# One strip of an expert transfer sent as sixteen transfers of eight rows, in a slot-attention, soft-MoE and softplus-MLP kernel

## The chip, the cores and the metric

The kernel runs on one core of a Trainium2 chip. The metric is the device time of one execution in microseconds (us): 570.08 us, the median of three runs (569.05, 570.08 and 570.2).

## The reference

Three blocks follow each other. An attention over 32 memory slots for each of 8 batches and 8 heads gives x of 4608 rows by 512. A soft mixture of eight experts then reads x through 32 slots, and each expert multiplies its four slots by two matrices of 2 MB each:

```python
slot_input = d.T @ x                      # d: softmax over all rows of x @ phi
for e in range(E):                        # E = 8
    h = np.maximum(slot_input[e] @ w1[e], 0.0)      # w1[e]: 512 x 1024
    slot_out[e] = h @ w2[e]                         # w2[e]: 1024 x 512
x = c @ slot_out                          # c: softmax over the slots
g = np.maximum(h, 0.0) + np.log1p(np.exp(-np.abs(h)))   # h = x @ w_in
return g @ w_out
```

The expert matrices are 32 MB, the largest input. They are multiplied with only 32 slot rows, so their cost is that of loading them.

## The kernel before

The kernel has three stages. In the first the attention is computed and reduced to the 32 slot inputs (`SX`). In the second the experts are applied. In the third, some 390 us long, the softplus MLP runs over all 4608 rows; TensorE's matrices there are built from `soT`, which comes out of the last product of the second stage.

The sixteen expert matrices lie in HBM in the order of their use, as eight blocks `moe_w[0]` to `moe_w[7]` of 128 rows by 8192 floats (4 MB, two matrices side by side, 32 KB in a row). `expert_loads` (L1052) brings each block into one of four buffers of 4 MB (`both`, the pool `w32`); blocks 0 to 6 are one transfer each, block 7 is four (2 MB, 1 MB, 512 KB and 512 KB). Block 4 holds `w1` of experts 4 and 5, and takes the buffer of block 0. All loads are issued by SyncE's queue (SP) in the order of the program: two pairs of MLP weights, the eight blocks, then the other MLP weights (L1109, L1118).

`first_layer` (L1278) computes an expert's hidden rows (`hid`, L1285) and transposes them (`hTp`, L1301); `second_layer` (L1309) adds its output to two banks of PSUM (`S`, L1318), in the order of the experts. The last of these products releases `slot_out` (`sop`, L1342), and with it the third stage (L1544 and after). Where the planner expected TensorE to wait, it put in products of zeros (`idle`, L956), a number that is fixed when the program is built.

The order of instructions on every engine is fixed by the planner `Flow`, which simulates times when the program is built. The transfers of SP take eight completion semaphores in turn (DMAHW0 to DMAHW7, called lanes here). SP starts a transfer on a lane only when the transfer before it on that lane, eight transfers back, has landed. These waits are written by the layer under the kernel and not in its text, and they stand in the program's order.

Of the kernel before, what the change touches and what calls it, by code (L numbers as in the profile page):

```python
# [283 lines left out]
def tile_slot_attention_soft_moe_softplus_mlp(  # L284
# [10 lines left out]
    nc = tc.nc  # L295
# [698 lines left out]
    for pr in range(NPR):  # L994
        r = 20 * pr
# [56 lines left out]
    def expert_loads():  # L1052

        order = [(w, e + i) for e in range(0, NE - 4, 2) for w in ("w1", "w2") for i in range(2)]
        order += [("w1", NE - 4), ("w1", NE - 3), ("w2", NE - 4), ("w1", NE - 2)]
        order += [("w1", NE - 1), ("w2", NE - 3), ("w2", NE - 2), ("w2", NE - 1)]
        for n in range(NE):
            pair = order[2 * n : 2 * n + 2]
            ends = [0, 8192] if n < NE - 1 else [0, 4096, *(4096 + y for _, y in LAST_PARTS)]
            for a, b in zip(ends, ends[1:]):  # L1060
                yield [("D", 0.03 + 9.7 * (b - a) / 8192)], [] if a else ["+w32"], 0
                if a == 0:
                    i = flow.got["w32"]
                    both = w32[i].tile([128, 8192], F32, tag="w32", name="w")
                    for k, (kind, e) in enumerate(pair):
                        at[kind, e] = i
                        views(kind, e, both[:, 4096 * k : 4096 * k + 4096])
                nc.sync.dma_start(out=both[:, a:b], in_=moe_w[n][:, a:b])
                for k, (kind, e) in enumerate(pair):
                    arrived_w(kind, e, a - 4096 * k, b - 4096 * k)  # L1070

# [10 lines left out]
    def views(kind, e, t):  # L1082
        if kind == "w1":
            for n in range(2):
                w1_t[e, n] = t[:, 2048 * n : 2048 * n + 2048].rearrange("p (k f) -> p k f", k=KC)
            return
        for n in range(2):
            w2_t[e, n] = t[:, 2048 * n : 2048 * n + 2048].rearrange("p (h k d) -> p h k d", h=2, k=4)

    def arrived_w(kind, e, a, b):  # L1090
        if kind == "w1":
            done(f"w1{e}")
            return
        for n in range(2):
            for half in range(2):
                if a <= 2048 * n + 1024 * half < b:
                    done(f"w2{e}{n}.{half}")
# [28 lines left out]
    def weight_loads():  # L1126
        early = list(EARLY)
        for _ in range(early_at.count(-1)):
            x = early.pop(0)
            yield from load_wi(x[1]) if x[0] == "wi" else load_wo(x[1])  # L1130
        yield from expert_loads()
        for x in early + LATE:
            yield from load_wi(x[1]) if x[0] == "wi" else load_wo(x[1])
# [129 lines left out]
    def runs(units):  # L1263

        n = len(groups(units))
        if n == 1:
            return [(q, 0) for q in "1265734"]
        return [("2", 0), ("1", 0), ("2", 1), ("1", 1), ("3", 0), ("3", 1), ("6", 0), ("6", 1)] + [
            ("5", 0), ("7", 0), ("7", 1), ("5", 1), ("4", 0), ("4", 1)
        ]  # L1270
# [640 lines left out]
    n = 0  # L1911
# [8 lines left out]
    for j, (where, units) in enumerate(JOBS):  # L1920
        if isinstance(where, int):
            for u in units:
                r = due[j, u] - LEAD["h"] - 1e4 * (n == 0)
                flow.add(first_h(n, list(last_h)), r, "fb")
                r = due[j, u] - LEAD["g"] - 1e4 * (n == 0)
# [14 lines left out]
        r = due[j, runs(units)[0][0], 0] - LEAD["x"]  # L1940
# [104 lines left out]
```

## Time and profile before

| | |
|---|---|
| median of three runs | 570.08 us |
| the profiled execution | 569.04 us |
| its span | 567.3 us |
| PE busy | 544.3 us, 96% of the span |
| DVE busy, ACT busy | 461.4 us, 373.5 us |
| DMA from SP | 96.80 MB |

The span is cut into 40 slices of 14.2 us in the page's second part; a digit is the busy share of a slice in tenths. PE is TensorE, DVE VectorE, ACT ScalarE, SPq the queue of SyncE that issues transfers, PEld TensorE's load of the stationary matrix. A transfer's time to landing runs from the start of its issue to its completion.

### The profile page before, as it was taken

Reading aid. Unit: us, or ns where it says so; the run is one execution under the profiler, and the core shown is the slowest. Engines: PE = TensorE matmul, PEld = TensorE weight load, DVE = VectorE, ACT = ScalarE, POOL = GpSimd, SP = SyncE. Lnnn points to the kernel's source line nnn. Section 1 sums busy time; section 2 is a strip of 40 time slices with the busy share of each in tenths; the row PEclk is TensorE's granted clock in tenths of the full one; section 3 lists DMA queues with packets and bytes.
Section 4 is the critical chain, followed back from the end, with each engine's and each line's share of the span. In section 5 each row is a group of like instructions: output and inputs, shape, how many; then the busy total and the mean of one; then the engine's idle time right before and its main releaser. Section 6 shows DMA issues by size and latency. Waiting matters only on the chain.

```text
span 567.3 us, 10017 instructions
## 1 busy us (share of the span) xinstructions
PE 544.3 (96%) x4054; PEld 418.2 (74%) x4062; DVE 461.4 (81%) x596; ACT 373.5 (66%) x527; POOL 61.1 (11%) x76
## 2 busy tenths in 40 slices
PE   8789989998799999999999999999999999999997
PEld 4556766544447888888888888888888888888885
DVE  4578989888815998999999999999999758778953
ACT  3567866334413898588967976886887976765520
POOL 1000000000000001001023121322112110211100
PEclk9899999999899999999999999999999999999999
DMA  8999999999999476558599876899669554766842
GB/s 354 429 418 433 415 420 438 427 429 432 424 411 406 176 222 150 194 158 185 230 221 151 158 125 103 150 153 182 99 101 157 92 87 74 118 113 119 160 87 111
DMA packets 22078, 132.05 MB, mean 233 GB/s; under 512 B 2960, under 2 KB 4624, under 8 KB 16656
## 3 DMA queue, kind: packets, MB, share of 16 engines
q1 hardware_dynamic: 12528, 96.80, 41.7%
q0 software_dynamic: 9504, 34.61, 36.4%
q8 instruction: 32, 0.52, 0.4%
q14 instruction: 14, 0.11, 0.1%
HBM read 85.00 MB, written 42.47 MB: 225 GB/s over the span
## 4 chain that ended last, share of the span: by engine, by line
PE 87%; DVE 5%; DMA 3%; ACT 2%; issue 1%; SPq 0%; DVEq 0%; ACTq 0%
PE ob L1837 53%; PE ob L1691 8%; PE hp L1718 5%; DMA kv<-in_kv_dram 3%; PE idle L956 3%; PE kvp L529 3%; PE rp L609 2%; PE tp L712 2%; PE S L1318 2%; PE sc L648 1%; PE tp L484 1%; PE ob L1865 1%; PE U L859 1%; DVE arena L1192 1%; ACT a L628 1%
## 5 line engine op out<-in xcount | busy, mean ns | idle before, releaser
L1837 PE MATMUL ob<-g,WS 128*128 128x512 f32 x768 | 181.8, 389 | 0.0
L1837 PEld LDWEIGHTS ob<-g,WS 128*128 128x128 f32 x768 | 144.0, 188 | 30.2 <-issue 0.4
L1837 PE MATMUL ob<-g,W 128*128 128x512 f32 x552 | 130.5, 389 | 0.0
L1837 PEld LDWEIGHTS ob<-g,W 128*128 128x128 f32 x552 | 103.5, 188 | 21.7 <-ACT outs L837 0.2
L837 ACT ACTIVATE outs<-ob 128x1024 f32<-128x1024 f32 x78 | 80.2, 1028 | 51.4 <-PE ob L1837 40.7
L1479 POOL DMA_DIRECT2D out_dram<-outs x60 | 53.1, 919 | 451.2 <-ACT g L1782 203.0
L1784 DVE TENSOR_TENSOR g<-arena,g 128x1024 fp32r<-128x1024 f32 x61 | 74.1, 1221 | 19.7 <-ACT g L1782 19.6
L1782 ACT ACTIVATE g<-arena 128x1024 fp32r<-128x1024 f32 x61 | 64.3, 1057 | 16.6 <-PE ob L1837 13.7
L1691 PE MATMUL ob<-g,W 128*128 128x512 f32 x192 | 46.4, 390 | 0.0
L1472 DVE TENSOR_TENSOR outs<-ob,outs 128x1024 f32<-128x1024 f32 x30 | 36.7, 1223 | 11.0 <-PE ob L1837 10.8
L1691 PEld LDWEIGHTS ob<-g,W 128*128 128x128 f32 x192 | 36.0, 188 | 7.4
L1718 PE MATMUL hp<-CT,Gs 128*128 128x512 f32 x128 | 38.6, 390 | 0.0
L1784 DVE TENSOR_TENSOR g<-x,g 128x1024 fp32r<-128x1024 f32 x26 | 31.4, 1220 | 3.2 <-ACT g L1782 3.1
L956 PE MATMUL idle<-zero 128*128 128x512 bf16 x111 | 29.9, 403 | 2.5 <-POOL zero L959 1.5
L1784 DVE TENSOR_TENSOR g<-room,g 128x1024 fp32r<-128x1024 f32 x25 | 30.1, 1220 | 2.0 <-ACT g L1782 2.0
L1782 ACT ACTIVATE g<-x 128x1024 fp32r<-128x1024 f32 x26 | 27.5, 1058 | 4.4 <-PE ob L1837 2.3
L1782 ACT ACTIVATE g<-room 128x1024 fp32r<-128x1024 f32 x25 | 26.4, 1058 | 5.1 <-PE ob L1837 4.4
L1731 ACT ACTIVATE arena<-hp 128x1024 f32<-128x1024 f32 x30 | 29.6, 1019 | 0.0
L1718 PEld LDWEIGHTS hp<-CT,Gs 128*128 128x128 f32 x128 | 23.9, 188 | 5.1 <-issue 0.2
L529 PE MATMUL kvp<-kv,et 128*32 128x128 f32 x512 | 20.1, 289 | 3.0 <-DMA kv<-in_kv_dram 3.0
L956 PEld LDWEIGHTS <-zero 128*128 128x128 bf16 x119 | 11.3, 103 | 13.8 <-issue 4.6
L653 DVE TENSOR_REDUCE smx<-sc 128x16 f32<-128x512 f32 (+1 forms) x20 | 12.6, 631 | 8.2 <-PE sc L648 8.0
(202 smaller groups left out, 731.7 us busy)
## 6 DMA issues: line engine op xcount, KB each, us to landing
out_dram<-outs POOLq DMA_DIRECT2D x60, 512.0 KB, 5.4
w<-in_moe_w_dram SPq DMA_DIRECT2D x7, 4096.0 KB, 20.8
kv<-in_kv_dram SPq DMA_DIRECT2D x6, 2880.0 KB, 20.7
out_dram<-outs SPq DMA_DIRECT2D x20, 512.0 KB, 3.1
wi<-in_w_in_dram SPq DMA_DIRECT2D x8, 1024.0 KB, 18.6
wo<-in_w_out_dram SPq DMA_DIRECT2D x8, 1024.0 KB, 16.3
q<-in_q_dram SPq DMA_DIRECT2D x4, 1280.0 KB, 20.2
q<-in_q_dram SPq DMA_DIRECT2D x4, 1024.0 KB, 20.5
```

Of the source, the lines that this page charges most:

```text
L529: nc.tensor.matmul(kvp[32 * h : 32 * h + 32], lhsT=rows[:, 32 * h : 32 * h + 32], rhs=rows_of[:, c, h] if c < SC else rest[:, h], start=(c ...
L653: nc.vector.tensor_reduce(out=mx[:, cc], in_=sc[:, : len(cs)], op=ALU.max, axis=AX.X)
L837: nc.scalar.activation(o, i, AF.Copy)
L956: nc.tensor.matmul(idle[0], lhsT=zero[:, :128], rhs=zero, start=True, stop=True)
L1472: nc.vector.tensor_tensor(out=o, in0=OB[at], in1=o, op=ALU.add)
L1479: nc.gpsimd.dma_start(out=place(half, tb), in_=o, accum_op=ALU.add)
L1691: nc.tensor.matmul(bank(oc), lhsT=W[u][:, w, i, c], rhs=hb[tb, u][:, x, i], start=(fresh and i == chunks[0] and k == "0"), stop=(stop and ...
L1718: nc.tensor.matmul(hp[:, i], lhsT=Gs[:, 128 * fc : 128 * fc + 128], rhs=CTf[:, TB * tb : TB * tb + TB], start=True, stop=True,)
L1731: nc.scalar.activation(X[key][:, m], hp, AF.Softplus)
L1782: nc.scalar.activation(g[:, 0], x, AF.Copy)
L1784: nc.vector.tensor_tensor(out=g[:, 1], in0=x, in1=g.bitcast(F32)[:, 0], op=ALU.subtract)
L1837: nc.tensor.matmul(OB[at][:, t], lhsT=(W if w == "W" else WS)[u][:, x, c, cols], rhs=g[:, y, m], start=(fresh and u == grp[0] and n == 0), ...
```

## The change

Block 4 is no longer one transfer. Its first 1024 floats of each row (4 KB of 32 KB, 512 KB in all) go as sixteen transfers of eight rows each: transfer r takes rows r, r+16, ..., r+112. The other 7168 floats of each row (3584 KB) follow as one transfer. The bytes and their places in the buffer are the same.

```diff
                 if a == 0:
...
                         views(kind, e, both[:, 4096 * k : 4096 * k + 4096])
+                if n == 4:
+                    for r in range(16):
+                        nc.sync.dma_start(out=both[r::16, :1024], in_=moe_w[n][r::16, :1024])
+                    a = 1024
                 nc.sync.dma_start(out=both[:, a:b], in_=moe_w[n][:, a:b])
+                a = a if n != 4 else 0
                 for k, (kind, e) in enumerate(pair):
                     arrived_w(kind, e, a - 4096 * k, b - 4096 * k)
```

On SP the program before has, from block 2 on, these rows; `w<-in_moe_w_dram` is a block or a part of one with its rows and floats, and the brackets hold the semaphores that the instruction waits for (DMAHW is a lane, PE, DVE and Activation are engines that must be done with the buffer).

```order
L1068 DMA w<-in_moe_w_dram 128x8192 [waits DMAHW2_49,PE_49]
L1068 DMA w<-in_moe_w_dram 128x8192 [waits DVE_49,PE_49,Activation_49]
L1068 DMA w<-in_moe_w_dram 128x8192 [waits DMAHW7_49,DMAHW3_49,PE_49]
L1068 DMA w<-in_moe_w_dram 128x8192 [waits DMAHW4_49,DMAHW1_49,PE_49]
L1068 DMA w<-in_moe_w_dram 128x8192 [waits DMAHW5_49,DMAHW0_49,PE_49]
L1068 DMA w<-in_moe_w_dram 128x4096 [waits DMAHW6_49,DMAHW2_49,PE_49]
```

The third row is block 4, on lane 3. Its neighbours count on from there: block 3, the second row, is on lane 2, blocks 2, 1 and 0 are on lanes 1, 0 and 7.

On SP the changed program has seventeen rows in the place of block 4. These are the last ten of them, from the eighth piece to the rest of the block, and the row of block 5.

```order
L1070 DMA w<-in_moe_w_dram 8x1024 [waits DMAHW2_49]
L1070 DMA w<-in_moe_w_dram 8x1024 [waits DMAHW3_49]
L1070 DMA w<-in_moe_w_dram 8x1024 [waits DMAHW4_49]
L1070 DMA w<-in_moe_w_dram 8x1024 [waits DMAHW5_49]
L1070 DMA w<-in_moe_w_dram 8x1024 [waits DMAHW6_49]
L1070 DMA w<-in_moe_w_dram 8x1024 [waits DMAHW7_49]
L1070 DMA w<-in_moe_w_dram 8x1024 [waits DMAHW0_49]
L1070 DMA w<-in_moe_w_dram 8x1024 [waits DMAHW1_49]
L1070 DMA w<-in_moe_w_dram 8x1024 [waits DMAHW2_49]
L1072 DMA w<-in_moe_w_dram 128x7168 [waits DMAHW3_49]
L1072 DMA w<-in_moe_w_dram 128x8192 [waits DMAHW4_49,PE_49]
```

The eighth piece (the first row) is on lane 2, the lane of block 3. The sixteenth piece (the last but two) waits for the eighth, the rest of block 4 for the ninth, and block 5 for the tenth. The seven pieces ahead of the first row wait for transfers up to block 2, and the first of them for the buffer, as block 4 did before.

On PE the first layer of expert 4 waited for one lane before; `hid<-w,room` is its product, `S_1883<-w,hT` and `ctp` are what stands before it.

```order
L1318 MATMUL S_1883<-w,hT 32x256 x4
L1255 MATMUL ctp<-ident,c_2111 128x128 [waits DVE_49]
L1255 MATMUL ctp<-ident,c_2111 128x128 x3
L1285 MATMUL hid<-w,room 32x256 [waits DMAHW3_49]
L1285 MATMUL hid<-w,room 32x256 x15
```

On PE in the changed program the same products wait for all eight lanes, at the same place in the order.

```order
L1323 MATMUL S_1883<-w,hT 32x256 x4
L1260 MATMUL ctp<-ident,c_2127 128x128 [waits DVE_49]
L1260 MATMUL ctp<-ident,c_2127 128x128 x3
L1290 MATMUL hid<-w,room 32x256 [waits DMAHW4_49,DMAHW5_49,DMAHW3_49,DMAHW6_49,DMAHW2_49,DMAHW7_49,DMAHW1_49,DMAHW0_49]
L1290 MATMUL hid<-w,room 32x256
L1290 MATMUL hid<-w,room 32x256 [waits DMAHW3_49]
L1290 MATMUL hid<-w,room 32x256 x13
```

Before, the first product waited for the one transfer on lane 3. Now the first waits for the strip, whose sixteen pieces are on all eight lanes, and the third for the rest of the block, on lane 3 too. The order of the other engines' instructions is the same as before.

## Rows read from the trace of the kernel before

**Rows 1.** The span in 40 slices, second part of the page.

```profile
PE   8789989998799999999999999999999999999997
...
PEclk9899999999899999999999999999999999999999
DMA  8999999999999476558599876899669554766842
GB/s 354 429 418 433 415 420 438 427 429 432 424 411 406 176 222 150 194 158 185 230 221 151 158 125 103 150 153 182 99 101 157 92 87 74 118 113 119 160 87 111
```

**Rows 2.** DMA queues from 80 to 180 us: packets, bytes, share of 16 engines.

```profile
DMA packets 2795, 42.53 MB, mean 425 GB/s; under 512 B 310, under 2 KB 310, under 8 KB 566
...
q1 hardware_dynamic: 2783, 42.35, 99.9%
```

**Rows 3.** SP's issues in order of time: start us, us, line, what, number.

```profile
108.08 0.33 SPq L1068 DMA_DIRECT2D w<-in_moe_w_dram  x1
...
126.04 0.33 SPq L1068 DMA_DIRECT2D w<-in_moe_w_dram  x1
...
133.28 2.05 SPq L1068 DMA_DIRECT2D w<-in_moe_w_dram  x2
...
142.97 1.75 SPq L1068 DMA_DIRECT2D w<-in_moe_w_dram  x4
...
144.29 0.43 SPq L1068 DMA_DIRECT2D w<-in_moe_w_dram  x1
...
240.74 5.27 SPq L1428 DMA_DIRECT2D arena<-gq  x8
```

**Rows 4.** Issues at 108.08, 126.04, 144.29 and 232.02 us: KB, us to landing.

```profile
w<-in_moe_w_dram SPq DMA_DIRECT2D x1, 4096.0 KB, 24.6
...
w<-in_moe_w_dram SPq DMA_DIRECT2D x1, 4096.0 KB, 16.3
...
w<-in_moe_w_dram SPq DMA_DIRECT2D x1, 512.0 KB, 28.6
...
arena<-gq SPq DMA_DIRECT2D x1, 16.0 KB, 1.8
```

**Rows 5.** What SP waited for: us in total, times, longest us.

```profile
SPq L1068 <- PE hTp L1301: 17.9, 1, 17.9
```

**Rows 6.** DMA issues of the whole span: KB each, median us to landing.

```profile
outs<-out_dram SPq DMA_DIRECT2D x3, 512.0 KB, 3.5
arena<-gq SPq DMA_DIRECT2D x48, 16.0 KB, 3.4
```

**Rows 7.** PE in order of time: start us, us, line, operation, shape, number.

```profile
143.43 1.93 PE L1285 MATMUL hid<-w,room 128*32 128x256 f32 x32
...
153.35 3.20 PE L1318 MATMUL S<-w,hT 128*32 128x256 f32 x32
...
160.16 3.83 PE L956 MATMUL idle<-zero 128*128 128x512 bf16 x17
...
169.78 3.84 PE L1318 MATMUL S<-w,hT 128*32 128x256 f32 x64
173.55 1.33 PE L1342 MATMUL sop<-sel,s2s 128*128 128x128 f32 x8
```

**Rows 8.** PEld at the end of the second stage, idle before in brackets.

```profile
172.98 0.16 PEld L1318 LDWEIGHTS S<-w,hT 128*32 128x32 f32 x8 [0.46 <-DMA w<-in_moe_w_dram]
```

**Rows 9.** Stretches: busy us (number) of five engines, PEclk, DMA share, GB/s.

```profile
149.00:152.00 3.00, 0.88 (x6) 0.64 (x6) 2.42 (x5) 1.23 (x4) 0.00 (x0) 1.00 1.05 442
152.00:154.00 2.00, 1.60 (x12) 1.02 (x16) 1.21 (x2) 1.65 (x3) 0.00 (x0) 0.64 0.99 426
154.00:156.00 2.00, 2.00 (x25) 0.87 (x20) 1.86 (x5) 0.05 (x1) 0.00 (x0) 0.51 0.91 393
...
174.00:200.00 26.00, 26.00 (x133) 22.06 (x132) 23.09 (x30) 18.52 (x27) 0.00 (x0) 1.00 0.68 275
...
300.00:560.00 260.00, 260.00 (x1202) 214.73 (x1201) 217.58 (x208) 184.53 (x196) 48.38 (x55) 1.00 0.70 120
```

## The prediction

> **What bounds the kernel now.** I read the span in slices first. In the first 13 of the 40 slices, to 184 us, the DMA row stands at 8 and then 9 and the rate mostly above 410 GB/s; behind them the rate falls to about half and less, while PE stands at 9 to the end [rows 1]. So a stage bound by loads is followed by one bound by TensorE. The DMA queues confirm the first half: from 80 to 180 us the 16 engines are 99.9% busy with SP's transfers, at 425 GB/s [rows 2]. The stretches confirm the second: from 174 to 200 us and from 300 to 560 us PE is busy for the whole of the stretch [rows 9]. Hence the end is set by the moment at which the third stage starts, plus work that has no gap to give back.
>
> That moment hangs on block 7. Its last part is issued at 144.29 us [rows 3] and lands 28.6 us later [rows 4], at 172.9. TensorE's last weight load of the experts is released by exactly this transfer, at 172.98 [rows 8], and the product `sop`, with which the third stage begins, follows at 173.55 [rows 7]. The products of zeros ahead of it, such as the 17 at 160.16 [rows 7], are no reserve: their number is fixed, and behind them the transfer is still what is waited for. So whatever the stream of expert blocks loses before 172.9 us comes out at the end, one for one.
>
> The block in question is issued at 126.04, when SP has waited 17.9 us [rows 3, 5] for TensorE to leave the buffer. Block 3, issued at 108.08 and landing 24.6 us later at 132.7, is then still moving; block 4 lands 16.3 us after its issue, at 142.3 [rows 3, 4]. The two landings are 9.66 us apart: block 4 was queued 6.7 us ahead of its turn, and the stream had no gap. 4096 KB in 9.66 us makes 2.36 us for 1024 KB, 1.2 us for the strip of 512 KB and 8.45 us for the rest of 3584 KB.
>
> **The change, part by part.** It removes one issue of SP and adds seventeen, and it adds a wait. No bytes are added, and no engine but SP and PE has another order.
>
> *The first seven pieces.* They follow from 126.04 on. What a transfer in a row costs on SP is shown from two sides: block 7's four parts take 1.75 us, 0.44 each, and eight transfers of 16 KB take 5.27 us, 0.66 each [rows 3]. So the seven are out between 129.1 and 130.7, behind block 3, and cost nothing; the stream hides them.
>
> *The eighth piece.* It is on block 3's lane and waits until that has landed, at 132.7. SP therefore stands for 2.0 to 3.6 us, and behind it in SP's order stand eight more pieces, the rest of block 4 and blocks 5 to 7. Nothing else is queued at the DMA engines but seven pieces of 32 KB, which is 0.5 us of the stream's rate. It is this wait that ends last now: the stream runs dry.
>
> *The pieces from the eighth on.* Nine issues lie between 132.7 and the issue of the rest. At 0.44 us they take 4.0, at 0.66 us 5.9, and if each took only its own 0.33 [rows 3], 3.0. I take 0.5, 4.5 in all: they are loads like block 7's parts, which gave 0.44, but nearly all wait on a lane as the small ones do. The rest goes out at 137.2. Two more lane waits stand in this stretch, of the sixteenth piece for the eighth and of the rest for the ninth; each has eight issues, 4.0 us, to be covered by, and a small transfer lands in 1.8 to 3.4 us [rows 4, 6]. They cost nothing; at 0.44 us and 3.4 us they would just fit.
>
> *Starting the stream again.* On a quiet queue 16 KB land 1.8 us after the issue [rows 4], and 512 KB take 3.5 us [rows 6], of which 1.2 is their transport: 2.3. So between 1.8 and 2.3 us are added to the 8.45; I take 2.0. The rest of block 4 then lands at 137.2 + 2.0 + 8.45 = 147.65, against 142.3: 5.3 us late. From both sides: 132.7 + 4.0 + 1.8 + 8.45 = 146.95, 4.6 late; 132.7 + 5.9 + 2.3 + 8.45 = 149.35, 7.0 late; with 0.33 us an issue 146.0, 3.6 late.
>
> *Behind it.* Blocks 5 and 6 were issued at 133.28 and some 1.7 us later, the first part of block 7 at 142.97 [rows 3]. They now follow the rest at 137.7 and 138.2 at the earliest, well ahead of their turn at 147, so the stream has one gap and no second, and each lands 5.3 us later than before, the last at 178.2.
>
> *TensorE.* `hid` of expert 4 starts at 143.43 now [rows 7] and would start at 147.7, with the few more semaphores that it waits for beside a wait that is longer anyway. A pause of four us can cost clock: after 149 to 152 us, in which PE was busy for 0.88 of 3 us, the granted clock is 0.64 and then 0.51, about 1.2 of 2.4 GHz [rows 9], and 32 products of `S` take 3.20 us, where 64 take 3.84 later [rows 7]. If the same befell `hid`, two experts' products would grow by 2.6 us. Block 5 comes 9.66 us after block 4, and 9.9 us lie between the starts of `hid` and `S` [rows 7], of which more than 2 us, in the stretch at 149, are waits that are over by then. So I cost it at nothing; without that cover it would be 1 to 2 us.
>
> **Sum.** The profiled execution took 569.04 us, of which 567.3 is the span; 569.04 + 5.3 = 574.3. It is 1.04 us under the median of the three runs, on which the sum is 575.4. Two of the three runs lie at the upper value, so I forecast 575.0.
>
> **The rivals.** *Few engines.* If a piece of eight rows does not use all sixteen engines, its bytes pile up on some. One engine moves 32 KB in 1.21 us (4096 KB on sixteen in 9.66). On eight engines a piece is 0.15 us, under the 0.5 between issues, and nothing changes. On two, the sixteen pieces take 9.7 us, to 142.4, and the rest ends at 150.8: 8.5 late, 578.6 on the median. On one, 19.4 us: 18 late, 588. The traces hold no transfer of under 32 rows, so nothing here decides it; but what SP sends in 128 rows keeps all sixteen busy [rows 2]. The Trainium skill's page "DMA: Bandwidth & Descriptors", section "Why a DMA increments its semaphore by 16 and not by 1", says that the number of engines is the largest up to 16 that divides the slowest dimension of both sides; that is eight here, and by it the sum stays as it is. No run here shows it. Chance of two or fewer engines: 7%.
>
> *Each piece pays its landing.* If the nine pieces go one after the other, each at 1.8 us, they take 16.2 us, and block 4 lands at 159.4: 17 late, 587. Against it: eight small transfers were issued in 5.27 us, each landing in 1.8 to 3.4 [rows 3, 4, 6], so they overlap. The same page, section "Rules for kernel authors", says of transfers under 64 KB that one pays mostly overhead, which speaks against the change in either case; by the order of SP it is the issue that is paid here, not the landing. Chance 4%.
>
> *No wait that binds: not slower.* If the eighth piece's lane is free in time, SP goes through its seventeen rows from 126.04 without a stop. The stream has no gap only if the rest goes out 1.8 us ahead of 132.7, by 130.9, which needs 0.30 us an issue over sixteen; then block 4 lands at 142.3 as before, and the time is 570.1. At 0.44 the rest leaves at 133.1 and lands 1 us late, 571.1. Against it stand the lane's order and the shortest issue of 0.33 [rows 3]. Chance 4%, half of it within 0.2%.
>
> *The delay is taken up.* Transfers 5.3 us late could find time to spare further on. The last weight load's wait for the last part [rows 8] and a third stage with PE busy throughout [rows 9] speak against it; what it would take is the whole 5.3, for 570.1. Chance 3%.
>
> **How the numbers follow.** The forecast with its bounds of 3.6 and 7.0 us has 82%: 572.7 (on the lowest run, 569.05) to 577.2 (on the highest, 570.2). I draw the range from 572.8 to 578.2, since the costlier cases are likelier than the cheaper. Within 0.2%, 1.1 us, which is about what a measurement can tell from no change, lie the taken-up delay and half of the free lane: 5%. Faster needs a gain for which no row shows a source: 1%. Slower: 94%.
>
> **What would show it.** The rows of SP: seven issues from 126 us on, a pause to 132.7 that DMA of block 3 ends, nine more in some 4.5 us, and the rest at about 137. The stretch from 133 to 139 should show the DMA share far below 1, with 425 GB/s again behind it. `hid` of expert 4 should start near 148, `sop` near 179, and the third stage should be as long as before. Wrong would be: no pause of SP ahead of the eighth piece, a stream without a gap, pieces that land 10 us and more after their issue, or a `sop` that is late by much less than block 4.

## The result, and the profile after

| | median us | runs, lowest to highest | profiled execution us | its span us |
|---|---|---|---|---|
| before | 569.57 | 4, 569.01 to 570.2 | 569.04 | 567.3 |
| changed | 577.62 | 4, 576.6 to 579.09 | 576.6 | 574.8 |

The ratio is 1.0143, with a 95% interval of 1.0113 to 1.0173: slower by 6.4 to 9.9 us. The forecast was 575.0 with a range of 572.8 to 578.2. The time lies in the range, 2.6 us above the forecast. The forecast stood on a base of 570.08 us, the median of three runs; with a fourth it is 569.57, so the change itself is 8.05 us on the medians and 7.6 on the profiled executions, against 5.3 in the prediction's sum.

The span in 40 slices of the changed kernel, second part of its page; a slice is 14.4 us now.

```profile
PE   8789989998689999999999999999999999999997
...
PEclk9799999999789999999999999999999999999999
DMA  9999999995999667465599956899678555666842
GB/s 362 425 424 427 417 419 438 430 414 176 432 425 410 278 196 207 171 200 123 164 294 158 180 96 109 149 161 169 114 119 146 78 93 86 111 106 118 164 90 110
```

In the tenth slice, from 129 to 144 us, the rate is 176 GB/s; the slices on either side are at 414 and 432, and before none of the first twelve but the opening one was under 410 [rows 1]. No other slice ahead of the third stage falls out of line. The place to look at is thus the tenth slice, and SP's rows show what happens there: start us, us, line, what, and their number, of the changed kernel (L1070 is the pieces, L1072 the whole transfers).

```profile
127.00 4.42 SPq L1070 DMA_DIRECT2D w<-in_moe_w_dram  x7
...
132.89 5.43 SPq L1070 DMA_DIRECT2D w<-in_moe_w_dram  x9
...
138.36 7.42 SPq L1072 DMA_DIRECT2D w<-in_moe_w_dram  x7
```

Seven pieces go out by 131.42; then SP stands until 132.89; then nine follow, and the rest of block 4 goes out at 138.36, where the whole block was issued at 126.04 before [rows 3]. (That the pieces start at 127.00 and not at 126.04 is not the change: in this execution the first stage was 1 us longer, in its repeat below 0.2 us. Block 3 lands 0.2 us later than before.) SP's waits from 100 to 180 us (what waited, for what, us in total, times, longest) name both causes; the first is the same as before [rows 5], the second is new.

```profile
SPq L1070 <- PE hTp L1306: 17.9, 1, 17.9
...
SPq L1070 <- DMA w<-in_moe_w_dram: 1.4, 1, 1.4
```

What the stream does meanwhile stands in stretches of 1 us of the changed kernel, in the columns of rows 9.

```profile
129.00:130.00 1.00, 1.00 (x24) 0.61 (x20) 1.00 (x3) 0.50 (x3) 0.00 (x0) 1.00 0.95 365
130.00:131.00 1.00, 1.00 (x26) 0.61 (x20) 0.96 (x3) 0.30 (x1) 0.00 (x0) 1.00 0.66 229
131.00:132.00 1.00, 1.00 (x17) 0.59 (x10) 0.96 (x2) 0.00 (x0) 0.00 (x0) 1.00 0.19 62
132.00:133.00 1.00, 1.00 (x19) 0.57 (x21) 0.97 (x2) 0.86 (x3) 0.00 (x0) 1.00 0.20 57
133.00:134.00 1.00, 1.00 (x24) 0.58 (x20) 1.00 (x2) 0.32 (x2) 0.00 (x0) 1.00 0.03 12
...
138.00:139.00 1.00, 1.00 (x24) 0.65 (x20) 1.00 (x3) 0.00 (x0) 0.00 (x0) 1.00 0.14 37
139.00:140.00 1.00, 1.00 (x19) 0.50 (x8) 0.73 (x1) 0.23 (x1) 0.00 (x0) 1.00 1.80 434
140.00:141.00 1.00, 0.50 (x5) 0.26 (x3) 0.14 (x1) 1.00 (x2) 0.00 (x0) 1.00 0.17 57
```

Read the last two columns, the DMA share and the rate. A packet, one row of a transfer, is counted whole in the stretch in which it starts; that is why the share is 1.80 at 139 and 0.17 behind it. So from about 131 to 139 us hardly anything but pieces is started. In the kernel before, the stream is full from 130 to 136 us:

```profile
130.00:132.00 2.00, 2.00 (x34) 1.16 (x30) 1.93 (x3) 0.82 (x3) 0.00 (x0) 1.00 1.08 451
132.00:134.00 2.00, 2.00 (x44) 1.23 (x40) 1.97 (x4) 0.74 (x3) 0.00 (x0) 1.00 0.95 410
134.00:136.00 2.00, 1.75 (x26) 0.93 (x18) 1.93 (x3) 0.43 (x1) 0.00 (x0) 1.00 1.03 442
```

The rate falls before SP is released at 132.89, because the sixteen DMA engines do not finish block 3 together. By the packets of the changed kernel's trace, block 3's last five of 32 KB start between 130.4 and 131.0 us and end between 131.6 and 132.4; its sixteen completion signals come from 128.98 to 132.87. In the kernel before they come from 129.12 to 132.63, but there an engine that is done goes on with block 4. Here it finds only pieces.

TensorE's rows of the changed kernel carry the delay to the third stage (start us, us, line, operation, shape, number, idle before and its releaser).

```profile
149.73 3.63 PE L1290 MATMUL hid<-w,room 128*32 128x256 f32 x28 [4.71 <-DMA w<-in_moe_w_dram]
...
160.75 3.53 PE L1323 MATMUL S<-w,hT 128*32 128x256 f32 x32 [1.80 <-DMA w<-in_moe_w_dram]
...
181.25 1.19 PE L1347 MATMUL sop<-sel,s2s 128*128 128x128 f32 x8
```

The weight load that waits for the last part of block 7, in the changed kernel:

```profile
180.46 0.24 PEld L1323 LDWEIGHTS S<-w,hT 128*32 128x32 f32 x8 [0.19 <-DMA w<-in_moe_w_dram]
```

The first layer of expert 4 resumes at 149.73, released by the transfer. The last weight load comes at 180.46 instead of 172.98 [rows 8], 7.5 us late, and `sop` at 181.25 instead of 173.55 [rows 7], 7.7 us late. From `sop` to the end of the span it is 393.55 us now and was 393.75. The third stage is as dense as before [rows 9]; the changed kernel's row:

```profile
300.00:560.00 260.00, 260.00 (x1202) 214.74 (x1201) 221.89 (x213) 190.53 (x202) 49.55 (x56) 1.00 0.73 126
```

So the whole difference of the spans, 7.5 us, is lost between 127 and 150 us and handed on unchanged.

### The profile page after: what moved, and what is told of

The parts are those of the page before. It is cut to its first block, busy times and chain, and to the rows that moved or that the text cites. A ratio compares the mean times of both kernels' runs of the same rounds, so it can differ in the third digit from the quotient of the medians.

```text
span 574.8 us, 10037 instructions
## 1 busy us (share of the span) xinstructions
PE 547.9 (95%) x4054; PEld 419.8 (73%) x4062; DVE 461.5 (80%) x596; ACT 373.5 (65%) x527; POOL 61.1 (11%) x76
## 4 chain that ended last, share of the span: by engine, by line
PE 84%; DMA 11%; SPq 1%; ACT 1%; DVE 1%; issue 0%; ACTq 0%
PE ob L1842 52%; DMA w<-in_moe_w_dram 8%; PE ob L1696 8%; PE hp L1723 5%; DMA kv<-in_kv_dram 3%; PE kvp L529 3%; PE idle L956 2%; PE rp L609 2%; PE tp L712 2%; PE S L1323 1%; PE sc L648 1%; PE tp L484 1%; PE ob L1870 1%; SPq L1070 1%; ACT a L628 1%; PE U L859 1%
## 5 line engine op out<-in xcount | busy, mean ns | idle before, releaser
L1290 PE MATMUL hid<-w,room 128*32 128x256 f32 x256 | 17.7, 409 | 5.2 <-DMA w<-in_moe_w_dram 4.7
L956 PEld LDWEIGHTS <-zero 128*128 128x128 bf16 x119 | 11.4, 104 | 14.3 <-issue 5.4
```

The lines of the kernel that those rows point to most:

```text
L956: nc.tensor.matmul(idle[0], lhsT=zero[:, :128], rhs=zero, start=True, stop=True)
L1290: nc.tensor.matmul(hid[32 * j : 32 * j + 32], lhsT=SX[:, kc, NS * e : NS * e + NS], rhs=w1_t[e, j // 2][:, kc, 256 * (j % 2) : 256 * (j % ...
```

## The experiments

The theory: a transfer of SP waits for the landing of the one eight places before it. The eighth piece therefore stops SP until block 3 has landed, and the loss is that stop, the issues queued behind it and the start of a dry stream. Its rivals: small transfers move slowly (few engines, or each paying its landing), and the number or the form of the pieces costs by itself, without any stop. All kernels below change the loop of the pieces alone; everything is still loaded. The kernel before, run beside each group of them, had medians of 569.69 to 569.86 us; each ratio is taken to its own.

### Four, eight and thirty-two pieces

`e4_four_pieces` puts 32 rows, 4 apart, into each piece:

```diff
-                    for r in range(16):
-                        nc.sync.dma_start(out=both[r::16, :1024], in_=moe_w[n][r::16, :1024])
+                    for r in range(4):
+                        nc.sync.dma_start(out=both[r::4, :1024], in_=moe_w[n][r::4, :1024])
```

> The strip goes as four transfers of 32 rows, so no piece is on the lane of block 3. Lane theory (the loss is SP's stop at block 3's lane, the issues behind it at 0.61 us each and the start of the dry stream at 2.9 us): the rest is issued near 129.5 us, ahead of block 3's landing, the stream has no gap, and the time is that of before within 0.2% (569 to 570.5 us). Rival, the strip itself costs (many short rows, small transfers at the DMA engines): 1 us or more is lost here too, 571 us and above.

Measured: 569.93 us, ratio 1.0005 (0.9996 to 1.0015): no loss. SP's row of this kernel shows four issues without a stop, and two stretches of it the stream going on where the changed kernel is dry.

```profile
125.89 2.48 SPq L1070 DMA_DIRECT2D w<-in_moe_w_dram  x4
```

```profile
130.00:132.00 2.00, 2.00 (x30) 1.18 (x26) 1.93 (x3) 0.97 (x3) 0.00 (x0) 1.00 0.90 342
132.00:134.00 2.00, 2.00 (x44) 1.19 (x40) 1.97 (x4) 0.59 (x2) 0.00 (x0) 1.00 1.06 449
```

`e8_eight_pieces` has `range(8)` and `[r::8]`, 16 rows each: the first count at which a piece meets block 3's lane.

```diff
+                    for r in range(8):
+                        nc.sync.dma_start(out=both[r::8, :1024], in_=moe_w[n][r::8, :1024])
```

> The strip goes as eight transfers of 16 rows; the eighth is on block 3's lane, and only it and the rest are issued behind the stop. Lane theory: rest at 132.9 + 0.6 = 133.5 us, landing 11.3 us later at 144.8, 2.5 us late; 572 to 573 us. Rival, few engines (pieces of eight rows load eight engines unevenly): 16 rows load all sixteen alike, so the loss is gone, 570 us. Rival, the strip itself costs: half of the loss with half of the pieces, 4 us, 573.5 us.

Measured: 573.32 us, ratio 1.0065 (1.0046 to 1.0084), 3.6 us slower, 0.3 us past what was expected. By the time alone the rival that half of the pieces cost half of the loss (573.5 us) fits as well or better; the rows speak for the stop:

```profile
SPq L1070 <- DMA w<-in_moe_w_dram: 3.7, 1, 3.7
```

The eighth piece goes out only at 134.28, 1.4 us later than the eighth of the changed kernel, because block 3 landed only then (134.26); a first sign that pieces can delay the block that is still moving. That delay is larger than the excess.

`e32_thirtytwo_pieces` has `range(32)` and `[r::32]`, 4 rows each: 25 issues behind the stop.

```diff
+                    for r in range(32):
+                        nc.sync.dma_start(out=both[r::32, :1024], in_=moe_w[n][r::32, :1024])
```

> The strip goes as 32 transfers of four rows. Lane theory: 25 issues stand behind the stop instead of nine, 16 more at 0.61 us, 9.7 us more than the changed kernel: 586 to 588 us. Rival, it is the landing of a round of eight lanes that is paid (2 to 2.9 us a round) and not the issues: two more rounds, 4 to 6 us more, 581 to 583 us. Rival, few engines: four rows on four engines, 128 KB each, 4.9 us of their time, hidden or not, 577 to 582 us.

Measured: 585.02 us, ratio 1.0269 (1.0254 to 1.0284), 15.3 us slower. It fits the issues one after the other, and is 2 us and more above what rounds of landings would give. SP's row of this kernel:

```profile
133.47 13.47 SPq L1070 DMA_DIRECT2D w<-in_moe_w_dram  x25
```

25 issues in 13.47 us are 0.54 each, somewhat shorter than the 0.61 of the changed kernel, which is why the time stayed a microsecond under the expectation's lower end.

### Sixteen pieces in other forms

`again_changed` is the changed kernel, unedited, run beside the experiments.

> The changed kernel as it is, on the chip of these experiments. Lane theory: 7.5 us over before (5.5 for nine issues at 0.61, 2.9 for the start of the stream, less the 1.2 of the strip, and some 0.3 later on): 576.5 to 577.8 us.

Measured: 577.58 us, ratio 1.0139 (1.0123 to 1.0154), 7.7 us slower. The result stands. Its trace differs in where the stop ends: block 3 lands at 133.59, the eighth piece goes out at 133.60, and nine issues of 0.61 us later the rest, at 139.07.

`e16w_wide_pieces` keeps sixteen pieces of 32 KB, each as 32 adjacent rows of 1 KB:

```diff
+                        rows, cols = slice(32 * (r % 4), 32 * (r % 4) + 32), slice(256 * (r // 4), 256 * (r // 4) + 256)
+                        nc.sync.dma_start(out=both[rows, cols], in_=moe_w[n][rows, cols])
```

> Sixteen pieces of the same 32 KB and on the same lanes, but of 32 rows by 256 floats (1 KB), so that the rows divide over all sixteen engines. Lane theory: the same stop and nine issues behind it; if an issue takes 0.56 us whatever its shape, 577 to 578 us as in the changed kernel; if it was long because of the eight rows and falls to the 0.44 us of the block's parts, 1.2 us less, 576 us. Rival, few engines: the loss is gone, 570 us.

Measured: 576.74 us, ratio 1.0129 (1.0111 to 1.0147), 7.05 us slower. Block 3 lands at 133.44, and the nine issues behind the stop take 5.1 us to the rest, about 0.46 us each but for one of 1.48. With 32 rows in a piece the loss stays, so it isn't that eight rows use few engines. The DMA engines from 134.0 to 134.8 us of the changed kernel, in which one piece moves, say how many a piece uses:

```profile
DMA packets 16, 0.03 MB, mean 41 GB/s; under 512 B 8, under 2 KB 8, under 8 KB 16
```

32 KB went as 8 packets of 4 KB, with 8 short ones, the signals: eight engines. By the rule that the prediction took from the Trainium skill's page "DMA: Bandwidth & Descriptors" (section "Why a DMA increments its semaphore by 16 and not by 1") it is eight as well, and the trace agrees.

`e16c_adjacent_rows` gives piece r the rows 8r to 8r+7 instead of rows 16 apart:

```diff
-                        nc.sync.dma_start(out=both[r::16, :1024], in_=moe_w[n][r::16, :1024])
+                        nc.sync.dma_start(out=both[8 * r : 8 * r + 8, :1024], in_=moe_w[n][8 * r : 8 * r + 8, :1024])
```

> Sixteen pieces of eight rows as in the changed kernel, but of adjacent rows (8r to 8r+7) and not 16 apart. Theory that the rows' spacing makes an issue long (0.56 us for rows 4, 8 or 16 apart, 0.42 for 32 adjacent rows): issues of 0.42 to 0.44 us, the nine behind the stop take 4.2 us and not 5.5, 1.3 us less than the changed kernel: 575.8 to 576.5 us. Rival, an issue is long because of the few rows: 0.56 us again, and the changed kernel's time.

Measured: 574.54 us, ratio 1.0088 (1.0073 to 1.0103), 4.7 us slower, better than expected. SP's row of this kernel shows why:

```profile
133.28 2.99 SPq L1070 DMA_DIRECT2D w<-in_moe_w_dram  x9
```

The stop ends within 0.4 us of the same place (132.89 in the changed kernel, 133.60 in its repeat), but an issue takes 0.34 us from start to start, not 0.61. Neither the theory's 0.42 to 0.44 nor the rival's 0.56 (each a piece's own duration) was right: it is 0.29 here. The nine cost 3.0 instead of 5.5 us, and the time is 3.0 us under that of the changed kernel beside it (577.58): 2.4 of the 3.0 are the issues. The bytes and the number of pieces are unchanged: what was paid in the changed kernel is, for the larger part, the issue on SP.

### Is it the stop, or the number of pieces?

`e6_six_pieces` was to stand just under the stop, `e7_seven_pieces` just on it (there the rest of block 4 is eight places behind block 3), with pieces of adjacent rows.

```diff
+                    cuts = (0, 16, 32, 48, 64, 96, 128)
+                    for x, y in zip(cuts, cuts[1:]):
+                        nc.sync.dma_start(out=both[x:y, :1024], in_=moe_w[n][x:y, :1024])
```

```diff
+                    cuts = (0, 16, 32, 48, 64, 80, 96, 128)
+                    for x, y in zip(cuts, cuts[1:]):
+                        nc.sync.dma_start(out=both[x:y, :1024], in_=moe_w[n][x:y, :1024])
```

> The strip goes as six transfers of adjacent rows (four of 16, two of 32), the rest is the seventh on lane 1 (block 2, landed at 122.9). Lane theory: no stop, the rest goes out ahead of block 3's landing, no gap: 569.3 to 570.5 us, the same as before. Rival, every piece costs its share of the loss (0.5 us each): 572.5 us.

> One piece more than with six (six of 16 rows, one of 32), so that the rest itself comes on lane 2 and waits for block 3. Lane theory: a stop with no issue behind it but the rest's; what is left is the start of the dry stream alone, 11.4 us from issue to landing against 9.66 without a gap, 1.7 to 2.2 us: 571.3 to 572 us. Rival, it is the number of issues alone, the stop being harmless: within 0.5 us of six pieces.

Measured: 572.71 us (ratio 1.0055, 1.004 to 1.007) with six, 572.88 (1.0061, 1.0044 to 1.0078) with seven. Both expectations failed. Six pieces should have cost nothing and cost 2.9 us; seven lie within 0.5 us of six, which was the rival's condition, although SP does stop in them (3.8 us, the rest at 134.31). SP doesn't stop in the six:

```profile
125.88 2.66 SPq L1071 DMA_DIRECT2D w<-in_moe_w_dram  x6
```

but the stream behind them is slow, in these stretches of the kernel with six:

```profile
130.00:132.00 2.00, 2.00 (x30) 1.19 (x26) 1.93 (x3) 0.98 (x3) 0.00 (x0) 1.00 0.91 252
132.00:134.00 2.00, 2.00 (x44) 1.21 (x40) 1.97 (x4) 0.58 (x2) 0.00 (x0) 1.00 0.96 227
```

The DMA share is over 0.9, as in a full stream, and the rate about half: the engines are busy, and each byte takes longer: the packets of 32 KB that start between 129.5 and 133 us take 1.96 us in the median, where they take 1.22 in the kernel before. Block 3 lands at 134.61, 2.0 us later than before. That is a second cost, which I had not seen, and it spoils this comparison of six and seven. It could lie in the number of pieces or in their narrow bands of adjacent rows. The next three kernels separate the two.

`x6_six_spread` and `x7_seven_spread` have the same numbers of pieces, but every piece takes rows 4 apart, all over the 128; to get to six or seven, some of the four groups of rows go in two halves.

```diff
+                    for r, x, y in ((0, 0, 1024), (1, 0, 1024), (2, 0, 512), (2, 512, 1024), (3, 0, 512), (3, 512, 1024)):
+                        nc.sync.dma_start(out=both[r::4, x:y], in_=moe_w[n][r::4, x:y])
```

```diff
+                    for r, x, y in ((0, 0, 1024), (1, 0, 512), (1, 512, 1024), (2, 0, 512), (2, 512, 1024), (3, 0, 512), (3, 512, 1024)):
+                        nc.sync.dma_start(out=both[r::4, x:y], in_=moe_w[n][r::4, x:y])
```

> Six pieces again, but each of 32 rows four apart (two of 1024 floats, four of 512), as in the four pieces that cost nothing. With six pieces of adjacent rows nothing stopped SP, and yet 2.9 us were lost: in its trace the stream runs at 227 to 315 GB/s from 130 to 136 us. Theory, SBUF's side: pieces whose rows lie close together are written by all sixteen engines into few parts of SBUF, and slow each other and the rows of block 3 down; with rows spread out this goes, and without a stop the time is that of before: 569.2 to 570.7 us. Rival, it is the number of pieces: 572.5 us as with six adjacent ones.

> Seven pieces of rows four apart, so that the rest waits for block 3's lane and nothing but the rest is issued behind the stop. Lane theory: landing 11.4 us after the issue at 132.9, 144.3, 2.0 us late: 571.4 to 572.4 us, against the time of before with six. Rival, the stop is harmless and only crowding counts: as with six, below 570.8 us.

Measured: 570.39 us with six (ratio 1.0014, 1.0005 to 1.0023), 571.55 with seven (1.0038, 1.0023 to 1.0053). Six spread pieces cost 0.7 us, where six adjacent ones cost 2.9: the number isn't what slowed the stream. One piece more costs 1.2 us, because the rest of the block itself now stops. SP's rows of `x6_six_spread`:

```profile
126.23 3.75 SPq L1070 DMA_DIRECT2D w<-in_moe_w_dram  x6
130.03 5.50 SPq L1072 DMA_DIRECT2D w<-in_moe_w_dram  x3
```

and of `x7_seven_spread`:

```profile
126.42 4.39 SPq L1070 DMA_DIRECT2D w<-in_moe_w_dram  x7
132.71 3.01 SPq L1072 DMA_DIRECT2D w<-in_moe_w_dram  x3
```

With six pieces the rest goes out at 130.03, right behind them. With seven it waits until 132.71, when block 3 has landed (132.69), though the pieces were all out by 130.8. SP's wait ahead of it and the first layer of expert 4, in `x7_seven_spread`:

```profile
SPq L1072 <- DMA w<-in_moe_w_dram: 1.9, 1, 1.9
```

```profile
145.12 1.92 PE L1290 MATMUL hid<-w,room 128*32 128x256 f32 x28 [0.70 <-DMA w<-in_moe_w_dram]
```

This is the stop by itself, with no issue queued behind it. The rest lands 12.4 us behind its issue, not 11.4 as expected, and 2.7 us later than block 4 before; but block 7's last part lands only 1.55 us later than before (174.49 against 172.94), and 1.9 us are lost in the time.

`e4c_four_adjacent` has the four pieces of the first experiment, which cost nothing, as bands of 32 adjacent rows:

```diff
+                    for r in range(4):
+                        nc.sync.dma_start(out=both[32 * r : 32 * r + 32, :1024], in_=moe_w[n][32 * r : 32 * r + 32, :1024])
```

> Four pieces of 32 adjacent rows, no stop. Theory of crowding: half of SBUF's parts for sixteen engines, so a piece's 4 KB take up to twice their 0.16 us; eight rows an engine, 1.3 us at most, 0.5 to 1.5 us lost: 570.2 to 571.3 us. Rival, the rows' spacing plays no part: 569.9 us as with four spread pieces.

Measured: 572.6 us, ratio 1.0056 (1.0039 to 1.0073), 2.9 us slower against 0.2 with rows 4 apart. Direction as expected, size double. The same bytes in as many pieces and no stop of SP ahead of the rest. Block 3's packets of 32 KB take 2.08 us in the median between 129.5 and 133 us, and 1.22 with rows 4 apart; it lands at 134.87, 2.2 us later; and the rate halves in three stretches of this kernel at a nearly full share:

```profile
130.00:132.00 2.00, 2.00 (x36) 1.16 (x29) 1.97 (x3) 0.38 (x1) 0.00 (x0) 1.00 0.94 231
132.00:134.00 2.00, 2.00 (x37) 1.23 (x39) 1.93 (x4) 1.18 (x3) 0.00 (x0) 1.00 0.83 203
134.00:136.00 2.00, 2.00 (x41) 0.99 (x33) 1.93 (x5) 0.39 (x1) 0.00 (x0) 1.00 1.07 262
```

`x16_sixteen_spread` asks whether this crowding has a part in the changed kernel's loss: sixteen pieces again, each of 32 rows 4 apart.

```diff
+                    for r, x, y in [(r, 256 * c, 256 * c + 256) for c in range(4) for r in range(4)]:
+                        nc.sync.dma_start(out=both[r::4, x:y], in_=moe_w[n][r::4, x:y])
```

> Sixteen pieces of 32 KB on the same lanes as in the changed kernel, of 32 rows four apart by 256 floats, on all engines and all parts of SBUF. Lane theory: nine issues of 0.63 us behind the stop, 5.7 us, and the start of the stream: block 4 lands 7.4 to 7.7 us late, 577 to 578 us, as the changed kernel. Rival, crowding of the eight-row pieces is a large part of the changed kernel's loss (as it was with six adjacent pieces, 2.9 us): 574 to 575 us.

Measured: 577.15 us, ratio 1.0137 (1.0122 to 1.0152), 7.5 us slower: the same as the changed kernel within its interval. The form that was free of crowding in four pieces changes nothing in sixteen, so crowding is no large part of the loss. A microsecond of it does hide there. Block 3 lands at 132.76 here and at 133.59 in the repeat of the changed kernel, 0.8 us later; but the nine issues take 6.4 us here and 5.5 there, one of them 1.36 us by itself (one of 1.44 stood in `e16w_wide_pieces`), and the two cancel.

### The kernels with a stop, side by side

| kernel | issues from the eighth piece on, us each | rest issued | `hid` resumes | between | slower by (medians) |
|---|---|---|---|---|---|
| changed | 9 at 0.61 | 138.36 | 149.73 | 11.4 | 8.05 |
| again_changed | 9 at 0.61 | 139.07 | 150.36 | 11.3 | 7.7 |
| e16c_adjacent_rows | 9 at 0.34 | 136.31 | 147.44 | 11.1 | 4.7 |
| e16w_wide_pieces | 9 at 0.57, one of them 1.48 | 138.54 | 150.15 | 11.6 | 7.05 |
| x16_sixteen_spread | 9 at 0.71, one of them 1.41 | 139.15 | 150.53 | 11.4 | 7.5 |
| e8_eight_pieces | 1 | 134.81 | 146.37 | 11.6 | 3.6 |
| e32_thirtytwo_pieces | 25 at 0.54 | 147.38 | 158.50 | 11.1 | 15.3 |
| x7_seven_spread | none | 132.71 | 145.12 | 12.4 | 1.9 |
| e7_seven_pieces | none | 134.31 | 146.71 | 12.4 | 3.0 |

Block 4 landed at 142.3 before [rows 4, by issue and duration]. In the first seven rows the time by which `hid` resumes behind that is the loss at the end to within a microsecond (16.2 against 15.3, 5.1 against 4.7, 4.1 against 3.6), and `hid` follows the issue of the rest by 11.1 to 11.6 us in every form. In the last two, where nothing but the rest is behind the stop, it follows by 12.4, and 0.9 and 1.4 us of the delay are not in the time. In both the last of the sixteen engines ends the rest 1.1 us behind the others, and while the rest moves the trace has 16 KB of another queue (0.9 to 1.0 us, from 137.91 in `x7_seven_spread`); in the other seven that starts ahead of the rest's first packet. That it is the cause is likely, not shown. So the moment at which the rest goes out sets the time, to about a microsecond.

No version beat the kernel before. The best ones, four or six spread pieces, come out level with it or 0.7 us behind.

## Why the prediction was right, and where its sizes were off

*What bounds the kernel* held: the delay of block 4 came out at the end one for one, 7.4 us where `hid` is released, 7.5 at the last weight load and 7.5 in the span.

*The first seven pieces* cost nearly nothing. They were dearer to issue than costed, 4.42 us or 0.63 each, so that SP stood for 1.4 us and not for 2.0 to 3.6; that made no difference, as block 3 ends the stop. But they aren't always hidden: block 3, at 132.6 before, landed at 132.9 in the changed kernel and at 133.6 in its repeat, and at 132.7 to 132.8 with pieces of rows 4 apart. The prediction put this at nothing; it is up to a microsecond.

*The eighth piece* does what was forecast, and this is shown: with six spread pieces the rest goes out at 130.03, with seven at 132.71, by a wait for DMA. The stop is what makes everything behind it visible.

*The pieces from the eighth on* was a mis-sized term. Its bounds held, the value in them did not. Nine issues took 5.47 us (132.89 to 138.36), 0.61 each, not 0.5: 1.0 us more. I placed the value near block 7's four parts, at 0.44; it lies near the other bound, the small stores at 0.66 [rows 3]. Those parts have 128 rows, the pieces eight rows 16 apart, and `e16c_adjacent_rows` shows that rows side by side would have given 0.34. I had taken the duration of an issue from what the transfer is for, where its form decides.

*Starting the stream again* was the other mis-sized term, and its bounds too narrow: 138.36 to 149.73 is 11.37, 2.9 over the transport of 8.45, not 1.8 to 2.3. The packets of the changed kernel's trace show where. None of the rest's has started by 139.42; all that start from 138 us on are pieces and signals:

```profile
DMA packets 37, 0.07 MB, mean 49 GB/s; under 512 B 20, under 2 KB 20, under 8 KB 37
```

The first starts at 139.44, 1.1 us behind the start of the issue. Fifteen of the first packets then take 1.6 to 2.3 us, where the later ones take 1.06 in the median; so the eight packets of an engine take 9.3 us on average and not 8.45, 0.9 more. The engines don't start and end together, which is another 0.5: the last packet ends at 149.30. The landing is seen 0.4 us behind that, at 149.69. I had bounded the start by 16 KB and 512 KB that land on a quiet queue [rows 4, 6], each a single number for everything but the transport; 3.5 MB on sixteen engines, each with a slow first packet, was outside of that. Why the first packets are slow stays open. The two terms make up 1.9 us of the 2.1 by which block 4 is later than forecast (149.73 against 147.65); block 3's landing adds 0.2.

The end of the range was luck in part. The dearest case of the forecast's own mechanism comes to 577.2 us, on the highest run; the measured median lies 0.4 above it, and two of the four runs lie above the range. The range held because 1 us was added for the costlier cases, with no term behind it.

*TensorE* behaved as costed. Its granted clock fell to 0.5, the lower of its two levels (1.2 of 2.4 GHz), behind a wait in which it had nearly nothing to do; the row of the changed kernel is

```profile
148.00:150.00 2.00, 0.27 (x4) 0.20 (x8) 1.93 (x3) 0.00 (x0) 0.00 (x0) 0.50 1.00 430
```

and 28 products of `hid` took 3.63 us. Yet the next expert's `S` at 160.75 still waits 1.80 us for its block, so the loss of clock is covered.

*Few engines* fell by the eight packets and by `e16w_wide_pieces`; *each piece pays its landing* by `e32_thirtytwo_pieces`, whose 25 issues are 0.54 us apart; *no wait that binds* and *the delay is taken up* by the rows above.

## What to carry to other kernels

A transfer that is cut into more pieces than the queue's lanes allow ahead of the one still moving makes the issuing engine stand; count the transfers back to the one that hasn't landed before cutting. What such a stop costs is less the wait, which the moving transfer covers in part, than what is queued behind it, and then the start of a dry stream, here 2.9 us over the transport. If a transfer like this one has to be cut, keep the pieces few enough, and spread each over all the rows; where many must be issued behind a stop, pieces of few adjacent rows were the cheapest to issue.

## What the runs showed of the hardware that I had not expected

The issue of a transfer on SP takes longer or shorter by its form: 0.29 us for 8 adjacent rows, 0.41 to 0.43 for 16 or 32 adjacent rows, 0.33 to 0.48 for 128, 0.50 for 4 rows 32 apart, and 0.56 to 0.59 for rows 4 to 16 apart (each its own duration in a row of issues, without the gap to the next and without the first of a row). Why spaced rows take longer stayed open.

A large transfer that is issued into a quiet stream starts slowly: its first packet came 1.0 to 1.2 us behind the issue in all nine kernels with a stop, and the landing 0.3 to 0.5 us behind the end of the last packet.

Pieces of 16 or 32 adjacent rows slow the stream beside them to 203 to 252 GB/s from 130 to 134 us with the engines still busy; the same bytes in rows 4 apart leave 342 and 449. The Trainium skill's page "SBUF — State Buffer", section "Door 1: The DMA port swizzle (why `[64,N]` ≈ `[32,N]`)", says that the DMA bandwidth depends on how many of 16 ports the partitions reach; by its table 32 adjacent rows reach half of them, rows 4 apart all. The direction agrees. The size isn't explained by it: 512 KB at half the rate would cost 1.2 us by estimate, and 2.9 were measured. Block 3's own packets of 32 KB slow down too, to 1.65 us in the median with rows 8 apart, 1.96 and 2.08 with adjacent ones, against 1.22 with rows 4 apart. But by the same table the changed kernel's eight rows, 16 apart, reach only four ports, yet with its first seven pieces those packets take 1.27 us, and block 3 was held up by 0.2 us and, in the repeat, by 1.0. That ports are the cause is therefore likely for the adjacent rows and not shown.
